# Linear attention into a routed attention layer: the last 64 tokens' values and scores by other shapes, and the whole program in another order

## The chip, the cores and the metric

The kernel runs on one core of a Trainium2 chip. The core has TensorE (PE in the profile, its weight loads PEld), VectorE (DVE), ScalarE (ACT), GpSimd (POOL), and SyncE (SP), which here issues all transfers. The metric is the device time of one execution in microseconds (us); of three runs the median counts.

## The reference

There are 8 batches of 576 tokens and 8 heads of 64. First comes a linear attention per head, with a feature map of 64 to 128, taken with both signs:

```python
def phi(x):
    proj = np.einsum('bhsd,df->bhsf', x, w_phi)
    proj = proj - np.max(np.abs(proj), axis=-1, keepdims=True)
    return np.concatenate([np.exp(proj), np.exp(-proj)], axis=-1)
q_p, k_p = (phi(q), phi(k))
kv = np.einsum('bhsf,bhsd->bhfd', k_p, v)
z = np.sum(k_p, axis=2)
num = np.einsum('bhsf,bhfd->bhsd', q_p, kv)
den = np.einsum('bhsf,bhf->bhs', q_p, z)[..., None] + 1e-06
return (num / den).astype(np.float32)
```

The heads' results side by side are x, 576 x 512 per batch. Then four experts of causal softmax attention (head width 64, scores scaled by 1/8) run on x, each with its own wq, wk, wv and wo. A token's result is the sum of its two best experts' outputs by `x @ w_gate`, weighted by a softmax over those two. All is float32.

## The kernel before

**Work.** Heads are handled in 32 pairs p (4 per batch), experts in two pairs g per batch b. A pair's queries and keys are projected with both heads' rows in the two halves of the array (`stream_q`, `stream_k`; the last 64 keys of both heads in `stream_tail`). Keys are centred on VectorE by their largest absolute value (`center`: a maximum and a subtraction) and turned into exponentials on ScalarE (`ek`). `stream_kv` sums keys by values into `kv`: 4 products (2 heads x 2 signs) of 65 columns (64 values and a one, for z), each over 5 blocks of tokens, in two 64-row halves. The fifth block holds the last 64 tokens of both heads, one head's in the upper partitions and the other's in the lower, and the values of the other head are zeros. Queries get their maximum from a POOL reduction (`phi_q`), a subtraction on VectorE and two exponentials on ScalarE; `stream_n` multiplies them by `kv`, `divide` divides, and `turn_x` transposes the quotients by way of memory into x.

**High and low parts.** x, the weights, q, k and y are kept as two float32r numbers, high and low, and a product is three: high by high, high by low, low by high. `proj_t` makes q and k of the expert pair g (`evac_q`, `evac_k`), `proj_v` the values and the gate's logits of all experts in 5 blocks of 128 tokens, the fifth of 64; `scores` the transposed scores in four steps n, 36 matmuls over 64 rows in all; `soft` masks them, copies them to `st`, and takes maxima; `post` subtracts and exponentiates them and multiplies by the values; `norm_y` and `move_y` scale and transpose; `project_out` (wo) and `store` end the batch. The key tile `kk2` is 640 columns wide, 64 of them zeros that `zeros` writes.

**Order.** Each of these is a generator of steps. `Plan.loop` walks through the string `PICKS`, two characters a step: the first picks the generator that goes on, the second the PSUM bank (of 8) that it gets, or, for a copy that ScalarE or VectorE can do, the engine. So `PICKS` sets every engine's order and the engine of every copy; each engine then works its own queue in that order and waits on semaphores. `keep_warm` issues matmuls of a constant, whose results nobody reads, in groups of three.

## Time and profile before

| | |
|---|---|
| runs | 564.62, 565.3, 569.82 us; median 565.3 |
| profiled execution | span 563.5 us, from the first to the last instruction; its time is not listed apart from the span, and the median stands 1.8 us above it |
| TensorE | busy 551.8 us (98%), weight loads 518.7 |
| VectorE | 492.9 us (87%) |
| ScalarE | 391.2 us (69%) |
| POOL | 192.7 us (34%) |
| DMA | 69 MB, all engines about half busy |

Busy time counts an engine from an instruction's start to its end; TensorE's matmuls are pipelined, so that several are open at once, and what one costs is the distance from its start to the next one's. A row `x16` merges that many instructions of a kind that follow each other. A float32 matmul of the code is two instructions in the profile, a float32r or bfloat16 one is one. Line 180 is the helper of the 128-row matmuls, line 407 that of the half-width ones, lines 189 and 202 the two engines' copies; there the names of the tiles tell the place.

### The profile page before, as it was taken

To read this page: it belongs to the slowest core of one execution; us is meant where nothing else is said; L and a number is where in the kernel's file an instruction comes from. 1 tells how busy PE (TensorE), PEld (TensorE's weight loads), DVE (VectorE), ACT (ScalarE), POOL (GpSimd) and SP (SyncE) were. 2 spreads that over 40 slices of the span, in tenths; PEclk is the share of its full clock that TensorE was granted. 3 is DMA by queue.
4 is the path that set the end of the run, shared out by engine and by line. 5 is a ranking of instruction groups with operands and counts; after the bars stand their busy time and mean duration, and the time that the engine had idled before them with its cause. 6 is when DMAs were issued, how large, how long until landed. Compare 5 with 4: busy or idle time off the path is not lost.

```text
span 563.5 us, 22862 instructions
## 1 busy us (share of the span) xinstructions
PE 551.8 (98%) x9704; PEld 518.7 (92%) x9704; DVE 492.9 (87%) x1245; ACT 391.2 (69%) x737; POOL 192.7 (34%) x78
## 2 busy tenths in 40 slices
PE   8999899999999999999999999999999999999996
PEld 6888799999999999999999999999999999999996
DVE  5799988999998999898878998899988998896992
ACT  3978757877956666897755784877785865574673
POOL 4565082244220555233203525083522310202320
PEclk9999999999999999999999999999999999999999
DMA  6577655555554636526545644356553253414222
GB/s 169 145 186 200 171 153 118 154 124 122 150 133 102 181 87 177 140 71 180 126 93 141 163 144 98 85 136 170 141 112 65 62 134 80 112 47 105 66 85 85
DMA packets 124757, 70.63 MB, mean 125 GB/s; under 512 B 81520, under 2 KB 107504, under 8 KB 124656
## 3 DMA queue, kind: packets, MB, share of 16 engines
q1 hardware_dynamic: 124656, 69.18, 48.7%
q8 instruction: 76, 1.25, 1.0%
q14 instruction: 25, 0.20, 0.1%
HBM read 46.15 MB, written 23.00 MB: 123 GB/s over the span
## 4 chain that ended last, share of the span: by engine, by line
PE 88%; DVE 8%; ACT 2%; issue 1%; DMA 0%; SPq 0%; DVEq 0%; ACTq 0%
PE ps_c L180 39%; PE ps_c L407 30%; PE ps_c L359 11%; PE ps_c L626 7%; DVE st L744 1%; DVE pmax L393 1%; DVE ek L395 1%; ACT ek L191 1%; DVE u L508 1%; DMA wf<-in_wts_dram 0%; DVE xt L540 0%; DVE xq L438 0%; DVE kv L202 0%; ACT u L189 0%; DVE u L202 0%
## 5 line engine op out<-in xcount | busy, mean ns | idle before, releaser
L498 POOL PARTITION_ALL_REDUCE mx<-u x32 | 127.0, 3993 | 113.7 <-ACT u L189 74.3
L180 PE MATMUL ps_c<-xh,qk 128*128 128x320 f32 (+1 forms) x512 | 106.3, 299 | 0.2 <-ACT st L189 0.2
L191 ACT ACTIVATE ek<-ek 128x1152 f32<-128x1152 f32 x64 | 74.8, 1169 | 26.4 <-DVE ek L395 25.5
L180 PEld LDWEIGHTS ps_c<-xh,qk 128*128 128x128 f32 x512 | 83.2, 189 | 1.8 <-ACT st L189 0.5
L498 POOL PARTITION_ALL_REDUCE tops<-top x15 | 54.2, 3611 | 82.9 <-DVE top L658 70.5
L407 PEld LDWEIGHTS ps_c<-v_in,ek 128*64 128x64 f32 x2560 | 77.4, 137 | 5.1 <-issue 2.6
L407 PE MATMUL ps_c<-v_in,ek 128*64 128x65 f32 x2560 | 81.4, 222 | 0.5 <-ACT ek L191 0.4
L180 PE MATMUL ps_c<-xl,qk 128*128 128x256 f32 (+1 forms) x256 | 75.8, 296 | 0.0
L189 ACT COPY st<-ps_c 128x288 f32<-128x288 f32 (+1 forms) x120 | 51.4, 505 | 25.1 <-DVE ps_c L646 16.7
L407 PE MATMUL ps_c<-kv,mx 128*64 128x65 f32 x1152 | 62.5, 224 | 3.3 <-DVE kv L202 2.6
L744 DVE TENSOR_TENSOR st<-st,tops 128x1152 f32<-128x1152 f32 (+4 forms) x75 | 57.7, 826 | 4.5 <-POOL tops L498 4.4
L393 DVE TENSOR_REDUCE pmax<-ps_c 128x4 f32<-128x512 f32 (+1 forms) x96 | 51.1, 546 | 11.0 <-PE ps_c L407 5.6
L407 PE MATMUL ps_c<-kv,u 128*64 128x65 f32 x1152 | 59.5, 221 | 0.0
L180 PE MATMUL ps_c<-vg,xh 128*128 128x260 f32 (+1 forms) x320 | 59.0, 285 | 0.0
L407 PEld LDWEIGHTS ps_c<-kv,mx 128*64 128x64 f32 x1152 | 48.1, 137 | 8.0 <-DVE kv L202 1.9
L189 ACT COPY u<-ps_c 128x320 f32<-128x320 f32 (+3 forms) x125 | 42.6, 416 | 17.2 <-PE ps_c L359 15.2
L395 DVE TENSOR_TENSOR ek<-ps_c,pmax 128x512 f32<-128x512 f32 (+1 forms) x96 | 51.9, 553 | 2.8 <-issue 0.5
L191 ACT ACTIVATE st<-st 128x1152 f32<-128x1152 f32 (+3 forms) x60 | 48.5, 865 | 7.0 <-DVE st L744 6.6
L180 PE MATMUL ps_c<-yh,wo 128*128 128x256 f32 (+1 forms) x256 | 52.1, 298 | 0.0
L180 PEld LDWEIGHTS ps_c<-xl,qk 128*128 128x128 f32 x256 | 48.5, 189 | 0.1
L407 PE MATMUL ps_c<-vl,st 128*64 128x65 f32 x1500 | 47.6, 222 | 0.8 <-ACT st L191 0.7
L180 PEld LDWEIGHTS ps_c<-vg,xh 128*128 128x128 f32 (+1 forms) x320 | 47.6, 177 | 0.8 <-issue 0.3
(116 smaller groups left out, 1175.4 us busy)
## 6 DMA issues: line engine op xcount, KB each, us to landing
v_in<-in_v_dram SPq DMA_DIRECT2D x32, 320.0 KB, 4.1
q_in<-in_qt_dram SPq DMA_DIRECT2D x64, 144.0 KB, 3.5
xl<-xd SPq DMA_DIRECT2D x32, 288.0 KB, 3.1
out_dram<-ot SPq DMA_DIRECT2D x32, 288.0 KB, 2.9
k_in<-in_kt_dram SPq DMA_DIRECT2D x32, 160.0 KB, 3.4
...
xd<-xt SPq DMA_DIRECT2D x64, 64.0 KB, 2.1
```

The source lines that it names most:

```text
L180: nc.tensor.matmul(o, a, b, start=start, stop=stop, skip_group_check=True)
L189: nc.scalar.copy(o, i)
L191: nc.scalar.activation(o, i, func, **kw)
L359: nc.tensor.matmul(o, a, b, start=True, stop=True, skip_group_check=True)
L393: dve(n * 128, [mk], [pk]).tensor_reduce(out=m[:, us], in_=src, axis=AX.X, op=ALU.max, apply_absolute_value=True)
L395: dve(n * 128, [(f'ek{p % EKB}1', us.start)], [pk, mk]).tensor_tensor(out=ek2[p % EKB][:, 1, us, :], in0=src, in1=m[:, us].unsqueeze(2).to ...
L407: nc.tensor.matmul(o, a, b, start=start, stop=stop, skip_group_check=True)
L498: nc.gpsimd.partition_all_reduce(o, i, 128, op)
L508: dve(2 * S, [uk], [mk], port=True).tensor_tensor(out=U, in0=U, in1=M, op=ALU.subtract)
L626: nc.tensor.matmul(pp_[e][:, o:o + q1 - q0], kk2[k_][r, 128 * j:128 * j + 128], q2[q_][r, q0:q1], start=m == 0, stop=m == 2, skip_group_ch ...
L744: dve(2 * n, [sj[j]], [*key, mk], port=True).tensor_tensor(out=a, in0=a, in1=tops[x][0:m, :, 128 * j:], op=ALU.subtract)
```

## The change

- **Values of the last 64 tokens.** x's high and low parts now lie in one tile `xb`. Once the low part is there, SP copies its last 64 tokens, high and low side by side, into `xe`, 128 columns. The fifth value block multiplies `xe` by the weights' high and low parts, 8 matmuls over 128 rows in place of 12 over 64. The upper 64 rows of the result are the high part's, the lower 64 the low part's; `evac_v` copies the lower ones to `vlo` and adds on VectorE.
- **Kv product.** For the last block one matmul per sign and half takes both heads' values, 130 columns, into two places of the bank; the other head's zeros make it right.
- **Last scores.** Where only 64 keys are left, the weights are 64 columns wide, not 128; `kk2` loses its zeros, and `zeros` goes.
- **Warm-up.** 18 groups of three, each with a bank of its own, at fixed places of the order; the first four key projections stand behind certain groups.
- **Order.** `PICKS` is another string throughout.

```diff
@@ -30,7 +30,8 @@
 EKB = 2
 XT_RATE = 1.085
 IB = 2
-WARM = 0
+WARMS = 18
+WARM_AT = (7, 11, 14, 17)
 
 
 ORDER = (('p0', 'v0', 's0', 'p1', 's1'), ('p0', 's0', 'p1', 's1', 'v0'))
@@ -50,51 +51,51 @@
 PICKS = (
-    "BACACADAAAAAAAAAAAAAAAAAAAGRNANAGjNANANACAG1OAOAG5OAOAOABAAAFCPIPIEjQIPIPIPIEADANICACAAAAAAAAAAAAAAAAAAAAAAAAAAAAAG1PAPA"
...
+    "BABABABABABABABABABABABABADAAAGIOAGaBAFECAE1NIQAHAQABANANANAPAOAGPQAQAGQRAADPAADADOAADEAOIADDADjBAFPFyCAMAQASAMAEFRAJAPA"
...
 )
@@ -167,8 +168,10 @@
     done = plan.done
     plan.both = [pp.tile([128, 512], F32, name=f"ps_c{i}") for i in range(BANKS)]
     plan.free = set(range(BANKS))
+    warm = cp.tile([128, 128], BF16, name="warm")
+    nc.vector.memset(warm, 1.0)
     for t in plan.both:
-        nc.vector.memset(t[:, NJ * V1 - 1:NJ * V1], 0.0)
+        nc.vector.memset(t[:, NJ * V1 - 1:512], 0.0)
 
     def sb(name, shape, dt=F32):
         return cp.tile(shape, dt, name=name)
@@ -209,8 +212,6 @@
     def load(o, i, w, r=(), rate=90.0):
         nc.sync.dma_start(o, i)
 
-    warm = sb("warm", [128, 128], BF16)
-    nc.vector.memset(warm, 1.0)
     col, row = sb("col", [128, 128]), sb("row", [128, 32])
     nc.vector.memset(col[:, 0:1], 0.0)
     for k in range(7):
@@ -254,7 +255,9 @@
     xt = [sb(f"xt{i}", [128, 4, 32 * NJ]) for i in range(2)]
     for t in xq:
         nc.vector.memset(t[64:128, :, 128:160], 0.0)
-    xT = [[sb(f"x{p}{i}", [128, S], F32R) for p in "hl"] for i in range(PXB)]
+    xB = [sb(f"xb{i}", [128, 2, S], F32R) for i in range(PXB)]
+    xT = [[t[:, n] for n in range(2)] for t in xB]
+    xE = sb("xe", [128, NP, 128], F32R)
 
     st = [[sb(f"st{n}", [128, 2, w]) for n, w in enumerate((S, 512, 512))], [u[n][:, :, 0:w] for n, w in enumerate((S, 512, 512))]]
     top, tops = [sb("top", [128, 2, S]), mx[0]], [sb("tops", [128, 2, S]), mx[1]]
@@ -265,11 +268,12 @@
     for t in yq:
         nc.vector.memset(t[64:128, :, 128:160], 0.0)
     q2 = [sb(f"q{p}", [128, S], F32R) for p in "hl"]
-    kk2 = [sb(f"kk{p}", [128, KC], F32R) for p in "hl"]
+    kk2 = [sb(f"kk{p}", [128, S], F32R) for p in "hl"]
     vl = sb("vl", [128, NJ, 4, 66])
     nc.vector.memset(vl[:, :, :, 65:66], 1.0)
     nc.vector.memset(vl[64:128, NJ - 1], 0.0)
     lg = vl[:, :, :, 0]
+    vlo = sb("vlo", [64, 4, 65])
     ge = sb("ge", [128, 5, 4, 4])
     gt, gs = sb("gt", [128, 3, 5, 4]), sb("gs", [128, 2, 5])
     gw = sb("gw", [128, 5, 4])
@@ -325,19 +329,13 @@
     w_vg = split_w("vg", WVG, [ot[1]], wts[:, c_vg:c_vg + WVG], 520)
     w_wo = split_w("wo", WO, [ot[0]], wts[:, c_vg + WVG:])
 
-    def zeros():
-        for x in kk2:
-            yield Step('POOL')
-            nc.gpsimd.memset(x[:, S:KC].bitcast(F32), 0.0)
-        done.add(('w', 4))
-
     def keep_warm():
-        pk, ps = yield Step('PE', (), 'c')
-        while ('x', WARM, 0) not in done:
-            yield Step('PE')
+        for n in range(WARMS):
+            t = yield Step('PE', (), 'c')
             for _ in range(3):
-                mm(ps[:, 0:128], warm, warm, True, True, 128, pk, [])
-        plan.release('c', (pk, ps))
+                mm(t[1][:, 0:128], warm, warm, True, True, 128, t[0], [])
+            plan.release('c', t)
+            done.add(('warm', n))
 
     def load_k():
         for p in range(NPAIRS):
@@ -361,7 +359,7 @@
     def stream_k():
         for p in range(NPAIRS):
             x, need = k_in[p % IB], [(f'k_in{p % IB}', n) for n in range(2)] + ['wphi']
-            k0, k1, pp_ = yield Step('PE', need, 'c', lambda: ('load_k', p) in done and ('w', 0) in done, tiling=(64, 128), n=3)
+            k0, k1, pp_ = yield Step('PE', need, 'c', lambda: ('load_k', p) in done and ('w', 0) in done and (p >= len(WARM_AT) or ('warm', WARM_AT[p]) in done), tiling=(64, 128), n=3)
             for n in range(4):
                 for h, pk in enumerate((k0, k1)):
                     r = slice(64 * h, 64 * h + 64)
@@ -455,14 +453,15 @@
             i = p % EKB
             ek, ekk = ek2[i], [f'ek{i}0'] + [(f'ek{i}1', t) for t in (0, 4, 8)]
             kc, ps = yield Step('PE', ekk + [vk], 'c', lambda: ('phi_k', p) in done and ('load_v', p) in done, tiling=(128, 64))
-            for h in range(2):
-                for c in range(2):
+            for c in range(2):
+                for h in range(2):
                     o = V1 * (2 * h + c)
-                    for t in range(NJ):
-                        u_ = 4 * h + t if t < 4 else 8
+                    for t in range(4):
                         for m in range(0, 128, 64):
-                            column_mm(ps[m:m + 64, o:o + V1], ek[:, c, u_, m:m + 64], v_in[:, 4 * h + t if t < 4 else 8 + h, :],
-                                       t == 0, t == 4, kc, ekk + [vk])
+                            column_mm(ps[m:m + 64, o:o + V1], ek[:, c, 4 * h + t, m:m + 64], v_in[:, 4 * h + t, :], c + h + t == 0, False, kc, ekk + [vk])
+                for m in range(0, 128, 64):
+                    to = ps[m:m + 64, 0:4 * V1].rearrange("p (h c x) -> p h c x", h=2, c=2)[:, :, c]
+                    nc.tensor.matmul(to, ek[:, c, 8, m:m + 64], v_in[:, 8:10, :], start=False, stop=True, skip_group_check=True)
             done.add(('kv', p))
             st = Step(copies(4 * V1), [kc], pred=has('num', p - 2) if p > 1 else None, hot=True)
             yield st
@@ -556,6 +555,9 @@
         sub_lo(S, lo, lo.bitcast(F32), hi, f'xl{i}', [*xr, f'xh{i}'])
         for s0, s1 in PARTS:
             done.add(('x', p, s0))
+        yield Step('SP', [f'xl{i}'], pred=(lambda: ('pe', p // NP - 1) in done) if p >= NP else None)
+        load(xE[:, p % NP].rearrange("f (n s) -> f n s", n=2).bitcast(F32), xB[i][:, :, 512:S].bitcast(F32), 'xe')
+        done.add(('xe', p))
 
     def all_x(*ps):
         return lambda: all(('x', p, q_[0]) in done for p in ps for q_ in PARTS)
@@ -606,7 +608,13 @@
         def evac_v(j, m, kc, ps):
             st = Step(copies(260), [kc], hot=True)
             yield st
-            copy(st.eng, 260, vl[:m, j, :, 0:65], ps[:m, 0:260].rearrange("p (n d) -> p n d", d=65), [f'vs{j}'], [kc])
+            src = ps[:, 0:260].rearrange("p (n d) -> p n d", d=65)
+            if m == 128:
+                copy(st.eng, 260, vl[:, j, :, 0:65], src, [f'vs{j}'], [kc])
+            else:
+                copy(st.eng, 260, vlo, src[64:128], ['vlo'], [kc])
+                yield Step('DVE', [kc], hot=True)
+                nc.vector.tensor_tensor(out=vl[0:64, j, :, 0:65], in0=src[0:64], in1=vlo, op=ALU.add)
             plan.release('c', (kc, ps))
             done.add(('v', b, j))
 
@@ -623,7 +631,8 @@
                     for m, (q_, k_) in enumerate(((0, 0), (0, 1), (1, 0))):
                         for e, pk in enumerate((k0, k1)):
                             r = slice(64 * e, 64 * e + 64)
-                            nc.tensor.matmul(pp_[e][:, o:o + q1 - q0], kk2[k_][r, 128 * j:128 * j + 128], q2[q_][r, q0:q1],
+                            n_ = min(128, S - 128 * j)
+                            nc.tensor.matmul(pp_[e][0:n_, o:o + q1 - q0], kk2[k_][r, 128 * j:128 * j + n_], q2[q_][r, q0:q1],
                                              start=m == 0, stop=m == 2, skip_group_check=True)
                 for e, pk in enumerate((k0, k1)):
                     plan.spawn(soft(g, n, blocks, e, pk, pp_[e]))
@@ -666,17 +675,17 @@
             wvg = wsp["vg"]
             for j in range(NJ):
                 m = min(128, S - 128 * j)
-                kc, ps = yield Step('PE', [k for c in xk for k in c], 'c', has('av', b - 1, 1) if b else has('w', 2))
-                n = 0
-                for c in range(4):
-                    for x_, w_ in ((0, 0), (0, 1), (1, 0)):
-                        mm(ps[:m, 0:260], xs[c][x_][:, 128 * j:128 * j + m],
-                           wvg[w_][:, c * 260:(c + 1) * 260], n == 0, n == 11, 260, kc,
-                           [xk[c][x_], ('vg', w_)])
-                        n += 1
+                kc, ps = yield Step('PE', (), 'c', lambda: ('w', 2) in done and (not b or ('av', b - 1, 1) in done) and (j < NJ - 1 or all(('xe', NP * b + c) in done for c in range(NP))))
+                parts = [(xs[c][x_][:, 128 * j:128 * j + m], c, w_) for c in range(4) for x_, w_ in ((0, 0), (0, 1), (1, 0))]
+                if m < 128:
+                    parts = [(xE[:, c], c, w_) for c in range(4) for w_ in range(2)]
+                for n, (x_, c, w_) in enumerate(parts):
+                    mm(ps[:, 0:260], x_, wvg[w_][:, c * 260:(c + 1) * 260], n == 0, n == len(parts) - 1, 260, kc, [])
+                if m < 128:
+                    done.add(('pe', b))
                 plan.spawn(evac_v(j, m, kc, ps))
 
-        yield Step('PE', (), None, lambda: all_x(*range(b * NP, b * NP + NP))() and all(('w', i) in done for i in (0, 1, 4)))
+        yield Step('PE', (), None, lambda: all_x(*range(b * NP, b * NP + NP))() and all(('w', i) in done for i in (0, 1)))
         for part in ORDER[b == B - 1]:
             yield Step('PE')
             g = int(part[-1])
@@ -862,7 +871,7 @@
         load(out[b, 128 * t:128 * t + 128, :], ot[t % 2], ('out', b, t), oks)
         done.add(('out', 4 * b + t))
 
-    for gen in (load_phi(), keep_warm(), zeros(), load_k(), load_q(), load_v(), stream_k(), stream_tail(), stream_q(), weights(w_qk, ('w', 1)), weights(w_vg, ('w', 2)), weights(w_wo, ('w', 3)), stream_kv(), stream_n(), stream_s()):
+    for gen in (load_phi(), keep_warm(), load_k(), load_q(), load_v(), stream_k(), stream_tail(), stream_q(), weights(w_qk, ('w', 1)), weights(w_vg, ('w', 2)), weights(w_wo, ('w', 3)), stream_kv(), stream_n(), stream_s()):
         plan.spawn(gen)
     plan.loop()
     in_order(tc, plan.behind)
```

What the string moves, at three places. TensorE at the start of the program, before (`q_in` and `k_in` are queries and keys of the first two pairs, in two buffers; the 64x128 rows are the last 64 keys):

```order
L359 MATMUL ps_c_65<-q_in_109,wf 128x256
L359 MATMUL ps_c_66<-q_in_110,wf 128x320
L359 MATMUL ps_c_67<-q_in_110,wf 128x320
L359 MATMUL ps_c_62<-q_in_110,wf 128x256
L359 MATMUL ps_c_68<-q_in_110,wf 128x256
L180 LDWEIGHTS warm
L180 MATMUL ps_c_61<-warm 128x128
...
L407 MATMUL ps_c_63<-wf,k_in_107 64x128 x2
L359 MATMUL ps_c_64<-wf,k_in_107 128x128
```

and now:

```order
L357 MATMUL ps_c_64<-q_in_109,wf 128x256
L405 MATMUL ps_c_65<-wf,k_in_107 64x128 x2
L357 MATMUL ps_c_66<-wf,k_in_107 128x128
...
L357 MATMUL ps_c_67<-wf,k_in_107 128x128
L357 MATMUL ps_c_68<-q_in_110,wf 128x320
L357 MATMUL ps_c_62<-q_in_110,wf 128x320
L357 MATMUL ps_c_61<-q_in_110,wf 128x256
L357 MATMUL ps_c_63<-q_in_110,wf 128x256
L183 LDWEIGHTS warm
```

The first pair's keys came after the second pair's queries and three warm-up matmuls; now they come before them.

TensorE at the end of one batch's value projection, before (`vg` are the value and gate weights, `xh` and `xl` x's parts, the 64-row results the fifth block):

```order
L180 MATMUL ps_c_64<-vg,xh_154 64x260 x2
L180 MATMUL ps_c_64<-vg,xl_155 64x260
L180 MATMUL ps_c_64<-vg,xh_156 64x260 x2
L180 MATMUL ps_c_64<-vg,xl_157 64x260
L180 MATMUL ps_c_64<-vg,xh_146 64x260 x2
L180 MATMUL ps_c_64<-vg,xl_147 64x260
L180 MATMUL ps_c_64<-vg,xh_148 64x260 x2
L180 MATMUL ps_c_64<-vg,xl_149 64x260
```

and now, at the end of another batch's:

```order
L183 MATMUL ps_c_65<-vg,xb_146 128x260 x3
L183 MATMUL ps_c_65<-vg,xb_147 128x260 x3
L183 MATMUL ps_c_65<-vg,xb_148 128x260 x3
L183 MATMUL ps_c_65<-vg,xb_149 128x260 x3
L183 MATMUL ps_c_68<-vg,xe 128x260 x8
```

Twelve matmuls of the fifth block became eight, from one tile.

VectorE in the third batch, now, around the fifth value block and a group of scores (lines 205 are copies, 655 the masks, 667 the maxima, 507 the queries' subtraction, 617 the new addition):

```order
L205 COPY vl<-ps_c_64 128x4x65
L205 COPY vl<-ps_c_63 128x4x65
L655 TENSOR_TENSOR ps_c_61<-ps_c_61,mask 128x128
L655 TENSOR_TENSOR ps_c_65<-ps_c_65,mask 128x128
L205 COPY vlo<-ps_c_62 64x260
...
L205 COPY st_155<-ps_c_63 128x512
L667 TENSOR_TENSOR top<-ps_c_64,st_153 128x448
L507 TENSOR_TENSOR u_129<-u_129,mx_133 128x1152
...
L188 TENSOR_TENSOR xb_147<-xb_147 128x576
L617 TENSOR_TENSOR vl<-ps_c_62,vlo 64x4x65
```

Before, every copy of `vl`, `st` and `ot` stood on ScalarE; now 7 of 40, 15 of 120 and 17 of 64 stand on VectorE (and 14 more of `u`, 8 of `kkh`, 4 of x), 65 in all.

## Rows read from the trace of the kernel before

**Rows 1.** The page's first part: busy us, share of the span, instructions of each engine.

```profile
PE 551.8 (98%) x9704; PEld 518.7 (92%) x9704; DVE 492.9 (87%) x1245; ACT 391.2 (69%) x737; POOL 192.7 (34%) x78
```

**Rows 2.** Busy time by stretch: length, engines' busy us (instructions), granted clock, DMA share, GB/s.

```profile
0.00:10.00 10.00, 7.98 (x49) 5.86 (x50) 4.07 (x43) 4.08 (x9) 2.64 (x7) 1.00 0.61 161
20.00:80.00 60.00, 56.85 (x1267) 50.71 (x1264) 55.51 (x126) 47.67 (x74) 29.99 (x9) 1.00 0.68 178
30.00:60.00 30.00, 29.04 (x675) 25.61 (x675) 29.31 (x62) 24.41 (x38) 15.72 (x4) 1.00 0.74 187
80.00:500.00 420.00, 417.72 (x7517) 396.96 (x7517) 379.68 (x941) 297.27 (x561) 139.94 (x55) 1.00 0.50 123
500.00:563.00 63.00, 59.22 (x712) 56.64 (x710) 45.30 (x126) 36.03 (x84) 12.42 (x7) 1.00 0.30 86
```

**Rows 3.** What TensorE waited for: us in total, times, longest.

```profile
PE ps_c L450 <- DVE yq L438: 0.8, 1, 0.8
...
PE ps_c L359 <- DMA wf<-in_wts_dram: 0.7, 1, 0.7
```

**Rows 4.** TensorE's timeline, value blocks: start us, length, engine, line, operation, count.

```profile
86.21 0.41 PE L180 MATMUL ps_c<-vg,xh 128*128 128x260 f32 x2
86.45 0.29 PE L180 MATMUL ps_c<-vg,xl 128*128 128x260 f32 x1
86.58 0.40 PE L180 MATMUL ps_c<-vg,xh 128*64 128x260 f32 x2
...
87.89 0.28 PE L180 MATMUL ps_c<-vg,xl 128*64 128x260 f32 x1
```

**Rows 5.** TensorE's timeline, 64-column scores.

```profile
89.62 0.27 PE L626 MATMUL ps_c<-qh,kkl 64*128 64x64 f32 x2
89.73 0.28 PE L626 MATMUL ps_c<-ql,kkh 64*128 64x64 f32 x2
89.84 0.39 PE L626 MATMUL ps_c<-qh,kkh 64*128 64x320 f32 x2
```

**Rows 6.** Groups by form: count, busy us, mean ns, idle before and its releasers.

```profile
L407 PEld LDWEIGHTS ps_c<-v_in,ek 128*64 128x64 f32 x2560 | 77.4, 137 | 5.1 <-issue 2.6 <-ACT ek L191 0.5 <-ACT u L189 0.5
...
L646 DVE TENSOR_TENSOR ps_c<-ps_c,mask 128x128 f32<-128x128 f32 x128 | 31.6, 289 | 7.3 <-PE ps_c L626 6.4
...
L626 PEld LDWEIGHTS ps_c<-qh,kkh 64*128 64x128 f32 x192 | 19.8, 185 | 3.2 <-issue 1.1 <-ACT st L189 0.7 <-ACT vl L189 0.4
...
L202 DVE COPY u<-ps_c 128x320 f32<-128x320 f32 x5 | 2.2, 483 | 0.3 <-PE ps_c L359 0.3
L202 DVE COPY u<-ps_c 128x256 f32<-128x256 f32 x6 | 2.2, 416 | 0.0
```

**Rows 7.** TensorE's timeline, a kv product and a key projection.

```profile
17.73 2.55 PE L407 MATMUL ps_c<-v_in,ek 128*64 128x65 f32 x80
20.11 0.39 PE L407 MATMUL ps_c<-wf,k_in 128*64 128x128 f32 x4
...
90.68 1.08 PE L359 MATMUL ps_c<-wf,k_in 64*128 64x128 f32 x16
91.69 0.44 PE L407 MATMUL ps_c<-wf,k_in 128*64 128x128 f32 x4
```

**Rows 8.** TensorE's timeline, the start.

```profile
1.30 2.74 PE L180 MATMUL ps_c<-warm 128*128 128x128 bf16 x24 [1.30 <-DVE col L215]
4.76 4.21 PE L359 MATMUL ps_c<-q_in,wf 64*128 64x320 f32 x16 [0.72 <-DMA wf<-in_wts_dram]
...
10.98 2.52 PE L180 MATMUL ps_c<-warm 128*128 128x128 bf16 x42
```

**Rows 9.** VectorE's timeline: its first key maximum, and a run of masks.

```profile
10.09 0.29 DVE L393 TENSOR_REDUCE pmax<-ps_c 128x1 f32<-128x128 f32 x1 [4.34 <-PE ps_c L407]
...
90.12 1.73 DVE L646 TENSOR_TENSOR ps_c<-ps_c,mask 128x128 f32<-128x128 f32 x8 [0.83 <-PE ps_c L626]
```

**Rows 10.** DMA issues: queue, kind, count, KB each, median us to landing.

```profile
yl<-yd SPq DMA_DIRECT2D x56, 64.0 KB, 3.0
```

More of the change, by code (lines that the diff above doesn't have):

```diff
@@ new lines @@
+    "XAWAWAVAQAUAMAUAHAJAUARAUASAF6FOGAGANAPAPIDADAQAYAOASASABABAQAGAQATAPAJAEDKhXARATIJIKGVAGAVAVARAQAOASASAPAUAUAWAWAWAWAWA"
+    "WAGAKAKAKCKFTAUAVAVACAGAGASASAFPFmCALAWIWAVIUADQQANAFjTAF-QAVAUAGAWAMAVAVAVARAVAOAOANANALAGAKAAAQANAQAOAJBJEJAJDQASARARA"
+    "QAJGJHJDJAJARAJqDADAOAPADMSIQATARASAJ3SAQARASATAJQJrJAWAWAXATAYAWAYAUALALAOASAUAUASASASAQAUAKAJGXAKAUAJBJHSASAPATARAVARA"
+    "WAJEVAGAECRASAWARAPAAABAVAUADADASAAADIHFEDQAPABAHAPATARATANAQAMACARAQAQADAHCHAOALAAAOALAOAOAEGQADAOADsOAIBOAITOAOAVAPAPA"
@@ new lines @@
+    "QAQAQACAMAGAPAO3PAOAOADADAQAQAQAHFQASAAASASAOAQAQAOALARARIHAMAOAOIQAOAMAJAJcJ6JBXATAQAXASIWARARATAUARAOAI1QAOAUARAHDRATA"
+    "RATALATARATIEEVARAHAFXUARAVAFdFhVAUARAPAVAVAOATIJCUARAVARAUAD9FZaAOAUATAXATAZAUANANAXASAXASASAUAPARACADAJADAMAJANABABALA"
+    "GAD0MAQAJDJBJHJCTATAOAEAPAIlTAXAXAVAPAQALAVAVAHCVAVAUATATAPAOASAHASASASASISAFHVISIRAMAQASAFZSAFqFHVAAAUADAOAOAVAOADADMOA"
+    "OAEFOAIWXAQASACAHAAANAYAYAXAVABAKAJAVAHIUAUASANAN7UASAGASASISASIJBJAJEJFJGQAOADALADATARATAPATAMASATATAQATITARAMAQALAOACA"
@@ L98 @@
+    "CACAGADAEIEABABGEADADABECICAABADDICABAAHACDABABIBAAFAAAGABAAAIAAAIAAAA"
 )
```

79 lines of the change are left out of this document (35 added, 44 removed).

## The prediction

> **What bounds the kernel now.** I read the page's busy shares first, then the busy times by stretch, then what TensorE waits for, then the timeline at each place that the change edits, and last the durations by form. The busy shares [rows 1] put TensorE at 98% and VectorE at 87% of a span of 563.5 us. The stretches [rows 2] tell more: from 80 to 500 us TensorE is idle 2.28 us out of 420, while VectorE is busy 379.68 (90.4%) and ScalarE 297.27 (71%). From 30 to 60 us it is VectorE that is full (29.31 of 30 us, 97.7%) and TensorE that loses 0.96 us. TensorE's waits are small: two of the list [rows 3] matter below, and only 0.7 us in the whole run is for a transfer. So after the start each matmul that goes away shortens the run, as long as VectorE can follow.
>
> **Values of the last 64 tokens.** Before, 12 matmuls of 260 columns with 64-wide weights begin at 86.58, the last of them at 87.89 [rows 4]: 1.31 us for eleven steps, 0.119 each. After, 8 of 260 columns with 128-wide weights do the work (the fourth product, low by low, comes along unasked). The 128-wide ones just ahead, three from 86.21 to 86.58, take 0.123 each. So 12 x 0.119 - 8 x 0.123 = 0.45 us per batch, 3.6 us in 8 batches, all on TensorE's path. The rows fix this within 0.5 us.
>
> **Last scores.** The six 64-column matmuls of a group come in pairs; the second pair starts at 89.62, the third at 89.73, the next form at 89.84 [rows 5]: 0.11 us per pair, though 64 columns are a quarter of the 260 that take 0.12. The pair waits for its two weight loads. A 128-wide load lasts 185 ns, a 64-wide one 137 [rows 6]. I take these two pairs as half as long, which saves 0.11 us per group and 1.8 over 16 groups. Ends: 0 if it isn't the load that holds them, 2.6 if all 96 matmuls gain 27 ns. The Trainium skill ("TensorE: Matmul & The Clock Gate", Step-by-step) says that a load's time scales with its column count; by that rule alone all loads halve, the saving is the 2.6, and the total would be 0.8 us lower. The rows show 185 against 137, less than half off, and the rows decide.
>
> **Kv product.** Per pair of heads, 80 instructions of 65 columns (two for each matmul of the code) take 2.38 us, 17.73 to 20.11 [rows 7], 30 ns each. Now 64 of 65 columns and 8 of 130 do it. By columns nothing changes. The nearest wide row of the same number type is the key projection: 16 of 128 columns in 1.01 us, 90.68 to 91.69, 63 ns each [rows 7], so 130 columns cost 64, against 2 x 30: a loss of 4 ns x 8 x 32 = 1 us at one end. At the other, if the loads set the pace, 8 x 30 ns x 32 = 7.7 us less. I take 0, near the projection's row.
>
> **The start.** Of 126 warm-up matmuls 54 are left: 39 at first (24 before) and 15 later (102 before, in runs of 42, 3 and 6). A run of 42 takes 2.52 us [rows 8], 60 ns each: 87 fewer are 5.2 us. The 15 more at the front stand ahead of the transfer that TensorE waits for anyway (0.7 us [rows 3]). What counts is whether something was ready in their place. VectorE idles 4.34 us until 10.09 [rows 9], since the first key projection stands behind the second pair's queries; in the new order the keys come right after the first pair's queries, and their transfer is issued ahead of the second queries. The second pair's queries, half of the 4.21 us at 4.76 [rows 8], and three warm-ups stood between: some 2.5 us that VectorE, the full engine of 30 to 60 us, starts earlier. With a little of the warm-up runs I take 3.0. Ends 0 and 5.2.
>
> **The end.** TensorE sits 0.8 us for the last transposes' input [rows 3]. Six output matmuls now stand in front of the transposes and fill part of it: 0.6 us. Ends 0 and 0.8.
>
> **Transfers.** Each pair adds a 64 KB copy into the new tile, on SP, which waits there for the low parts from VectorE; input and x transfers stand behind it in that queue. A 64 KB one lands in 3.0 us [rows 10], and TensorE paid 0.7 us for transfers in all. Only the fifth value block needs the copies, after four others of 12 x 0.12 us. I cost them at nothing; if that cover fails, it is about 2 us once per batch. The two small clears on POOL that go away were done before TensorE had data.
>
> **VectorE is what gets dearer.** Counting both orders, 65 copies go from ScalarE to VectorE: 20 of 320 columns, 18 of 256, 11 of 288, 5 of 512, 7 of 260 and 4 casts of 576. VectorE's rows give 483 ns for 320 columns and 416 for 256 [rows 6]; by the slope between them, 1.05 ns a column, the others are 450, 684, 420 and 752. That is 31.5 us. The new sum of the two halves adds 8 operations and 2 copies of 260 columns, 4.2 us. Against it 19 small ones leave, 6.1 us by their means. Net 29.6 us in 56 more instructions, whose ends overlap the next by some 60 ns (eight masks of 289 ns [rows 6] run in 1.73 us [rows 9]): 26 to 30, taken as 27, since casts out of SBUF run shorter than the slope says. The 492.9 becomes 520.
>
> **The sum.** TensorE's side: 563.5 - 3.6 - 1.8 - 0 - 3.0 - 0.6 = 554.5 us of span. VectorE's side: by 500 us it has done 447.6 (492.9 less 45.3), 4.1 of it before 10 us [rows 2]. Of the 27, 24 fall here. So 467.5 us must go between about 7 us and 63 us before the end; on TensorE's side that is 484.5 us, a level of 96.5%. The rows have 97.7% where VectorE is full and 90.4% where it had time to spare. So it just fits, and I add 1.0 for TensorE's waits (the 0.96 lost in the full 30 us; ends 0, and 13 if 3.2% were lost throughout, as from 30 to 60). Span 555.5. The runs' median, 565.3, stands 1.8 above this execution's span, so the forecast is **557 us**, 1.5% under the median.
>
> **Rivals.** *VectorE's level eats the gain.* The span is 467.5 / level + 70. At 95.8% the time is 559.6, where faster by 1% ends; at 95% it is 564, at 94.6% 566. For it: each engine works its queue in order, and from 20 to 80 us VectorE reached only 92.5% on average [rows 2]. Against it: much of that stretch is the start, where TensorE had warm-ups and little to feed VectorE with. Chance 0.27, 560 to 571.
>
> *VectorE's late copies stall TensorE, and the run gets slower.* The score, value and output copies that now queue on VectorE behind subtractions of 1152 columns hold PSUM banks, and the next matmuls wait for a bank. At the 92.5% of 20 to 80 us the span is 575 and the time 577. It decides from 93.7% downward. Against it: 105 of 120 score copies stay on ScalarE, which is 71% busy. Chance 0.07.
>
> *More is gained:* the start gives 5.2 and part of the kv loads' 7.7 comes true. Time 545 to 551, chance 0.08.
>
> *The clock falls.* The granted clock is 1.00, the 2.4 GHz level, in each stretch [rows 2]; but the first 24 warm-ups took 2.74 us and 42 later ones 2.52 [rows 8]. Without warm-ups after the first ones, the start's waits lie open as idle time. At half the clock some 20 us of matmuls there would cost up to 10 more: 567, chance 0.03. The Trainium skill's same page (HAM oscillation) says that gaps between bursts of matmuls drop the array to half its clock; no row here shows a fall before the tail.
>
> That the 64-wide loads save nothing moves the time by 1.8 only.
>
> **How the numbers follow.** The forecast, 551 to 559.6, has 0.55. One per cent is about what a measurement of this kernel can tell from no change; it ends at 559.6 and 571. Faster: 0.55 + 0.08 = 0.63. Same: 0.27 + 0.03 = 0.30. Slower: 0.07. The range reaches from 549 (half of the extra gain) to 566 (VectorE at 94.6%) and leaves out some 0.17.
>
> **What would show it.** Right: the last value block's eight matmuls in 0.98 us, the 64-column score pairs 0.055 apart, the first key maximum on VectorE before 8 us, VectorE near 520 us busy and over 96% from 20 us to 60 before the end, TensorE idle under 4 us from 80 to 490. Wrong: TensorE's waits for copies of VectorE or ScalarE over 6 us in sum, a granted clock below 1.00 before the tail, or VectorE well under 96% while TensorE isn't full.

## The result, and the profile after

The changed kernel takes 547.3 us (median of 4 runs, 545.87 to 549.14) against 565.6 for the kernel before: a ratio of 0.9666, with a 95% interval from 0.9626 to 0.9706. The forecast was 557, from 549 to 566. The direction was right, but 18 us came off where 8 were forecast. The profiled execution took 546.13 us with a span of 544.3.

The page's first part, against [rows 1]:

```profile
PE 532.4 (98%) x9344; PEld 506.3 (93%) x9344; DVE 501.5 (92%) x1301; ACT 373.6 (69%) x689; POOL 192.6 (35%) x76
```

TensorE is again at 98%, though the span is 19 us shorter: that share told nothing of what could be gained. VectorE has 501.5 us and not the 520 of the forecast. The busy times by stretch, against [rows 2]:

```profile
0.00:10.00 10.00, 8.71 (x88) 7.47 (x89) 8.05 (x49) 3.35 (x7) 2.29 (x5) 1.00 0.60 169
20.00:80.00 60.00, 57.69 (x1195) 53.34 (x1191) 54.49 (x117) 48.82 (x86) 35.47 (x9) 1.00 0.75 188
30.00:60.00 30.00, 28.77 (x750) 26.54 (x744) 27.40 (x65) 28.02 (x45) 13.42 (x5) 1.00 0.80 200
80.00:480.00 400.00, 395.73 (x7134) 380.08 (x7136) 375.82 (x975) 280.26 (x515) 136.81 (x54) 1.00 0.52 130
```

From 30 to 60 us VectorE is no longer the full engine: 27.40 us busy where it had 29.31, and ScalarE has 28.02 where it had 24.41. From 80 to 480 us VectorE is at 94.0% and TensorE idle for 4.27 us. The start on TensorE's timeline, against [rows 8]:

```profile
1.29 4.32 PE L183 MATMUL ps_c<-warm 128*128 128x128 bf16 x39 [1.29 <-DVE ps_c L174]
5.54 1.38 PE L357 MATMUL ps_c<-q_in,wf 64*128 64x320 f32 x8
6.84 0.44 PE L405 MATMUL ps_c<-wf,k_in 128*64 128x128 f32 x4
7.21 1.16 PE L357 MATMUL ps_c<-wf,k_in 64*128 64x128 f32 x16
8.21 1.14 PE L357 MATMUL ps_c<-q_in,wf 64*128 64x320 f32 x8
9.28 1.01 PE L183 MATMUL ps_c<-warm 128*128 128x128 bf16 x15
```

and VectorE's first maximum, against [rows 9]:

```profile
7.63 0.28 DVE L391 TENSOR_REDUCE pmax<-ps_c 128x1 f32<-128x128 f32 x1
```

The maximum comes at 7.63 us instead of 10.09, as forecast. The last value block and the 64-column scores, against [rows 4, 5]:

```profile
78.79 1.13 PE L183 MATMUL ps_c<-vg,xe 128*128 128x260 f32 x8
79.85 0.40 PE L635 MATMUL ps_c<-qh,kkh 64*128 64x288 f32 x2
...
82.25 0.21 PE L635 MATMUL ps_c<-qh,kkh 64*64 64x64 f32 x2
82.28 0.24 PE L635 MATMUL ps_c<-qh,kkl 64*64 64x64 f32 x2
82.33 0.24 PE L635 MATMUL ps_c<-ql,kkh 64*64 64x64 f32 x2
82.39 0.41 PE L635 MATMUL ps_c<-qh,kkh 64*128 64x320 f32 x2
```

The block's eight matmuls take 1.06 us (0.98 forecast); three score pairs take 0.14 us, 0.03 to 0.06 apart (0.055 forecast).

A first view of where the time went is the first expert projection, the first work that needs a whole batch of x. Its first row in the kernel before, and in the changed one:

```profile
74.29 0.38 PE L180 MATMUL ps_c<-xh,qk 128*128 128x256 f32 x1
```

```profile
62.36 0.86 PE L183 MATMUL ps_c<-xb,qk 128*128 128x256 f32 x5
```

It starts 11.9 us earlier. From there to the end the spans leave 489.2 us before and 481.9 after. So of 19.2 us of span, 11.9 lie ahead of that projection and 7.3 behind it. A mark like this depends on what an order puts ahead of it: the first scores, a little later, come only 8.2 us earlier (88.09 and 79.85), and the part on the prediction goes by them.

### The profile page after: what moved, and what is told of

It reads as the page before. It is cut to its first block, busy times and chain, and to the rows that moved or that the text cites. A ratio compares the mean times of both kernels' runs of the same rounds, so it can differ in the third digit from the quotient of the medians.

```text
span 544.3 us, 22196 instructions
## 1 busy us (share of the span) xinstructions
PE 532.4 (98%) x9344; PEld 506.3 (93%) x9344; DVE 501.5 (92%) x1301; ACT 373.6 (69%) x689; POOL 192.6 (35%) x76
## 4 chain that ended last, share of the span: by engine, by line
PE 83%; DVE 6%; DMA 5%; ACT 2%; SPq 2%; issue 1%; DVEq 0%; ACTq 0%
PE ps_c L183 38%; PE ps_c L405 26%; PE ps_c L357 11%; PE ps_c L635 7%; DMA xb<-xd 3%; PE ps_c L464 2%; SPq L213 2%; DMA xd<-xt 1%; DVE u L507 1%; DVE u L753 1%; DMA q_in<-in_qt_dram 1%; DVE pmax L391 1%; DVE ek L393 1%; DVE st L753 0%; ACT st L192 0%
## 5 line engine op out<-in xcount | busy, mean ns | idle before, releaser
L183 PE MATMUL ps_c<-xb,qk 128*128 128x256 f32 (+1 forms) x768 | 107.0, 297 | 0.5 <-DVE xb L188 0.4
L183 PEld LDWEIGHTS ps_c<-xb,qk 128*128 128x128 f32 x768 | 102.2, 188 | 2.7 <-DVE xb L188 0.9
L405 PE MATMUL ps_c<-v_in,ek 128*64 128x65 f32 x2048 | 72.0, 222 | 2.2 <-issue 1.4
L405 PEld LDWEIGHTS ps_c<-v_in,ek 128*64 128x64 f32 x2048 | 67.8, 137 | 4.4 <-issue 1.8
L192 ACT COPY st<-ps_c 128x288 f32<-128x288 f32 (+1 forms) x105 | 47.7, 506 | 24.6 <-DVE ps_c L655 17.8
L192 ACT COPY u<-ps_c 128x320 f32<-128x320 f32 (+3 forms) x111 | 40.7, 411 | 18.0 <-PE ps_c L357 16.8
L405 PEld LDWEIGHTS ps_c<-kv,u 128*64 128x64 f32 x1152 | 48.2, 138 | 0.0
L183 PE MATMUL ps_c<-vg,xb 128*128 128x260 f32 x384 | 48.0, 284 | 0.0
L183 PEld LDWEIGHTS ps_c<-vg,xb 128*128 128x128 f32 x384 | 46.7, 188 | 0.7 <-DVE ek L393 0.3
L405 PEld LDWEIGHTS ps_c<-vl,st 128*64 128x64 f32 x1500 | 45.6, 138 | 0.9 <-issue 0.6
```

What stands on the lines that cost most here:

```text
L183: nc.tensor.matmul(o, a, b, start=start, stop=stop, skip_group_check=True)
L192: nc.scalar.copy(o, i)
L405: nc.tensor.matmul(o, a, b, start=start, stop=stop, skip_group_check=True)
```

## The experiments

Each was timed beside the kernel before on the same chip; ratios are to that, with their 95% intervals, and a ratio need not be that of two medians. "Old order" is the string of steps of the kernel before, "new order" that of the changed one.

| kernel | us | ratio |
|---|---|---|
| changed kernel | 547.3 | 0.9666 (0.9626 to 0.9706) |
| new order, no edit of matmuls | 554.3 | 0.9784 (0.9741 to 0.9828) |
| old order, all three edits | 591.3 | 1.0476 (1.0432 to 1.0520) |
| new order, old kv | 550.1 | 0.9726 (0.9684 to 0.9767) |
| new order, old last scores | 549.8 | 0.9721 (0.9676 to 0.9767) |
| new order, old value block | 546.8 | 0.9663 (0.9619 to 0.9708) |
| old order, new kv and scores | 563.3 | 0.9966 (0.9927 to 1.0005) |
| old order, edits, sum on VectorE | 588.1 | 1.0395 (1.0345 to 1.0445) |
| the same, copies on GpSimd's queue | 566.6 | 1.0012 (0.9986 to 1.0038) |
| old order, edits, copies late | 605.2 | 1.0697 (1.0621 to 1.0772) |
| old order, 24 warm-ups | 568.6 | 1.0053 (1.0022 to 1.0083) |
| old order, keys first | 565.5 | 1.0003 (0.9967 to 1.0039) |
| old order, keys first, fewer warm-ups | 565.7 | 0.9999 (0.9973 to 1.0024) |
| new order, keys late | 548.7 | 0.9700 (0.9664 to 0.9736) |
| new order, 85 more warm-ups | 552.8 | 0.9788 (0.9748 to 0.9827) |
| new order, 15 fewer warm-ups | 548.0 | 0.9666 (0.9630 to 0.9702) |
| new order, 42 copies back on ScalarE | 557.4 | 0.9857 (0.9787 to 0.9926) |
| new order, score copies back | 553.8 | 0.9785 (0.9732 to 0.9837) |
| old order, the same 42 copies on VectorE | 589.2 | 1.0413 (1.0374 to 1.0453) |

**The order without the edits.** All three hunks on matmuls are undone; of each the core:

```diff
-                    for t in range(4):
+                    for t in range(NJ):
...
-                            n_ = min(128, S - 128 * j)
+                            n_ = 128
...
-                if m < 128:
-                    parts = [(xE[:, c], c, w_) for c in range(4) for w_ in range(2)]
```

> The new order with its warm-ups, but the old five-block kv product, 128-wide last scores and twelve-matmul last value block. Theory A (the order gives most of it, through the start): TensorE gets 7.1 us of matmuls back (kv 0.8, values 3.9, scores 2.5, by the spacing of the two traces), so 554 to 556 us, and the first expert projection still starts near 62 us. Theory B (the order gives what the prediction gave it, 3.6 us, the edits the rest): 561 to 563 us. Theory C (VectorE has taken over as the bound, matmuls are hidden): 547 to 549 us.

554.3 us, as in theory A. The order alone takes 12.2 us off by the ratio (9.7 to 14.6 by its interval; 10.6 by the medians, 9.1 by the spans of the two profiled executions), and the first expert projection starts at 63.52:

```profile
63.52 0.86 PE L183 MATMUL ps_c<-xb,qk 128*128 128x256 f32 x5
```

**The edits without the order.** The same three hunks, put into the kernel before; the 64 KB copy right behind the subtraction, the sum right behind the copy of the other half:

```diff
         sub_lo(S, lo, lo.bitcast(F32), hi, f'xl{i}', [*xr, f'xh{i}'])
+        load(xE[:, p % (2 * NP)]..., xB[i][:, :, 512:S].bitcast(F32), 'xe')
...
+                copy(st.eng, 260, vlo, src[64:128], ['vlo'], [kc])
+                nc.vector.tensor_tensor(out=vl[0:64, j, :, 0:65], in0=src[0:64], in1=vlo, op=ALU.add)
```

> The old order with all its 126 warm-ups, and the three edits (kv, last scores, last value block; the copies into the new tile have two sets of slots). Theory A: 7.1 us less matmul work, all on TensorE's path after the start, 557.5 to 559.5 us; the first expert projection still starts near 74 us. Theory B: the edits give 14 to 15 us, 550 to 552 us. Theory C (the old order can't use them, since VectorE is late at the start): 563 to 566 us.

No theory had this: 591.3 us, 26 slower. TensorE's list of waits in this run:

```profile
PE ps_c L409 <- DMA v_in<-in_v_dram: 4.1, 1, 4.1
PE ps_c L409 <- ACT kv L189: 3.2, 2, 2.7
PE ps_c L361 <- DMA q_in<-in_qt_dram: 3.0, 1, 3.0
```

and of SyncE's:

```profile
SPq L210 <- DVE xb L185: 40.1, 9, 11.3
```

SyncE stands 40.1 us for the low parts, and loads of values and queries come late. The granted clock is 0.98 here, where it was 1.00. Four runs followed this up.

**Kv and scores alone in the old order.**

```diff
-                    for t in range(NJ):
+                    for t in range(4):
...
+                            kk2[k_][r, 128 * j:min(S, 128 * j + 128)]
```

> The kernel before with the new kv product and the 64-column last scores, but its own last value block. The edits alone came out 26 us slower in the old order; this tells which of them does it. If the value block does (its copies, its sum of two halves): kv 0.8 and scores 2.5 us of matmuls go away on TensorE's path, 561 to 563 us. If any shortening of matmuls throws the old order out of step: over 573 us.

563.3 us, a gain of 1.9 whose interval still touches no change: of the three edits it is the value block, with its copies and its sum placed as here, that brings the loss.

**The sum without a wait for ScalarE.**

```diff
-                copy(st.eng, 260, vlo, src[64:128], ['vlo'], [kc])
+                copy('DVE', 260, vlo, src[64:128], ['vlo'], [kc])
```

> All three edits in the old order, the copies into the new tile behind the subtractions; of the last value block both halves go out on VectorE, so its sum waits for no copy of ScalarE. If VectorE's wait for that copy (7.9 us in six waits in the run of the edits alone) made the old order slow: 557 to 562 us. If the copies on SyncE's queue did, or the longer work on VectorE: 575 us or more.

588.1: VectorE's wait for the other half was at most a small part of it (3.2 us by the medians; the two intervals just overlap).

**The copies on another queue**, with the edit just shown kept:

```diff
-        load(xE[:, p % (2 * NP)]..., xB[i][:, :, 512:S].bitcast(F32), 'xe')
+        nc.gpsimd.dma_start(xE[:, p % (2 * NP)]..., xB[i][:, :, 512:S].bitcast(F32))
```

> All three edits in the old order, both halves of the last value block out on VectorE, and the 64 KB copies into the new tile issued from GpSimd's queue instead of SyncE's, so that the loads of values, queries and x stand behind no wait for VectorE. If SyncE's queue is what makes the old order lose (TensorE waits 4.1 us for values and 3.0 for queries in it): 558 to 563 us. If GpSimd now waits in its place (its maxima come later): 575 us or more.

566.6 us, 21.5 less by this line alone, though above the 558 to 563 expected. GpSimd stands for the low parts in SyncE's place (69.0 us in 12 waits), and neither loads of values nor of queries are in TensorE's list any more. The queue that waits for the low parts is shown as the cause. A part of the loss goes by way of the clock: its mean was 0.985 in the profiled execution of the run just shown and is 1.00 here, at most some 9 us by an estimate (0.015 of 587). That the edits still gain nothing here is not explained.

**The copies later on SyncE**, all four at the batch's first value block:

```diff
+                if j == 0:
+                    for c in range(NP):
+                        load(xE[:, (b * NP + c) % (2 * NP)]...)
```

> All three edits in the old order again, but the four 64 KB copies of a batch are issued together at its first value block, not each behind the subtraction that makes the low part. If the copies held up SyncE's queue (SyncE waits there for VectorE, loads of values and queries stand behind it): 557 to 561 us, and TensorE's waits for transfers under 1.5 us. If the sum of the two halves is the cause (VectorE waits there for a copy that stands in ScalarE's queue): 583 to 592 us.

A miss, 605.2: now the transfer itself is late, and the last block waits for it.

```profile
PE ps_c L180 <- DMA xe<-xb: 24.9, 5, 10.4
```

**Old kv product in the new order.**

```diff
-                    for t in range(4):
+                    for t in range(NJ):
```

> The changed kernel with the old kv product: five blocks of 65 columns per head and half instead of four and one of 130. By TensorE's spacing 0.8 to 1.8 us more, 548 to 549 us; at the forecast's price of nothing 547.3; if the weight loads set the pace, 7.7 more, 555 us.

**Old last scores in the new order.**

```diff
-    kk2 = [sb(f"kk{p}", [128, S], F32R) for p in "hl"]
+    kk2 = [sb(f"kk{p}", [128, KC], F32R) for p in "hl"]
...
-                            n_ = min(128, S - 128 * j)
+                            n_ = 128
```

> The changed kernel with 128-wide last scores (keys padded with zeros to 640). By the forecast's price 1.8 us more, 549; by TensorE's spacing 2.5 to 4.0, 550 to 551 us. If the value block's result repeats (3.9 us of matmuls that cost nothing in the whole): 546.5 to 548 us.

**Old value block in the new order.**

```diff
-                if m < 128:
-                    parts = [(xE[:, c], c, w_) for c in range(4) for w_ in range(2)]
...
-        load(xE[:, p % NP]..., xB[i][:, :, 512:S].bitcast(F32), 'xe')
```

> The changed kernel with the old last value block: twelve matmuls on 64 columns of x, no copies into the new tile, no sum of halves; the order is the same otherwise. By TensorE's spacing 3.9 to 4.6 us more, 551 to 552 us. If VectorE's relief (4.2 us of copy and sum less) outweighs it: 545 to 547 us.

Undone singly they cost 2.7, 2.5 and -0.5 us by the medians, all three undone together 7.0. An interval of one is some 3 us to either side, so only the three together are settled: they are near the 5.4 forecast. The value block, the largest of the forecast's edits (3.6), shows no gain of its own.

**Keys first, in the old order.** The order's rows on TensorE:

```diff
-L359 MATMUL ps_c_66<-q_in_110,wf 128x320
-L359 MATMUL ps_c_67<-q_in_110,wf 128x320
...
 L407 MATMUL ps_c_68<-wf,k_in_107 64x128 x2
 L359 MATMUL ps_c_66<-wf,k_in_107 128x128
...
+L359 MATMUL ps_c_62<-q_in_110,wf 128x320
+L359 MATMUL ps_c_63<-q_in_110,wf 128x320
```

> The kernel before with one piece of its order changed: the first pair's keys (their transfer, their matmuls, VectorE's maxima and subtractions of them) stand ahead of the second pair's queries; all 126 warm-ups stay. If this is the start's gain: VectorE's first maximum near 7.5 us instead of 10.1, the first expert projection 2.5 to 3 us earlier, 562 to 563 us. If it carries all of the start's 9 to 11 us: 555 to 557 us. If the 42 warm-ups that follow hide it: 565 us.

VectorE's first maximum comes at 6.71 us, 3.4 earlier, the first expert projection 2 us earlier, and the time is the same. The piece of the start on which the forecast rested shows no gain by itself; the interval leaves room for 1.9 us, less than the 2.5 that were given to it.

**Keys late, in the new order**: the same rows the other way round.

```diff
-L405 MATMUL ps_c_65<-wf,k_in_107 64x128 x2
...
+L357 MATMUL ps_c_66<-q_in_110,wf 128x320
```

> The changed kernel with the first pair's keys put back behind the second pair's queries (their matmuls and their transfer), banks dealt out anew for it; nothing else moves. If the early keys are worth what the prediction gave them: VectorE's first maximum 2 to 3 us later, the first expert projection at 64 to 65 us, 549.5 to 551 us. If they are worth nothing, as in the old order: 547 to 548 us.

548.7: 1.4 us, between the two cases and inside the intervals.

**Fewer warm-ups, old order.**

```diff
-            for _ in range(3):
+            for _ in range(3 if n <= 8 else 0):
```

> The kernel before with only the first 24 of its 126 warm-up matmuls; nothing else changes. If the warm-ups stood in the way of ready work: 102 x 60 ns = 6.1 us less, 559 to 560 us. If they only filled waits of the start (VectorE sets it): 564.5 to 566 us, with TensorE idle where they stood. If the clock falls in those gaps: granted clock under 1.00 before 80 us and 567 to 575 us.

The third case: 568.6, 0.5% slower, with two falls of the granted clock. Busy times by stretch in this run, and TensorE's timeline at the second fall:

```profile
68.00:70.00 2.00, 0.38 (x4) 0.00 (x0) 0.00 (x0) 1.01 (x2) 0.00 (x0) 1.00 0.23 53
70.00:72.00 2.00, 0.27 (x5) 0.30 (x7) 1.60 (x3) 1.80 (x4) 0.00 (x0) 0.67 0.02 8
72.00:74.00 2.00, 2.00 (x42) 2.00 (x41) 2.00 (x7) 0.52 (x2) 0.00 (x0) 0.50 0.71 200
74.00:76.00 2.00, 2.00 (x38) 1.88 (x36) 1.36 (x4) 1.14 (x4) 0.77 (x1) 0.50 0.61 155
76.00:78.00 2.00, 2.00 (x20) 1.97 (x22) 0.19 (x1) 0.00 (x0) 2.00 (x1) 0.62 0.59 133
78.00:80.00 2.00, 2.00 (x15) 1.04 (x13) 2.00 (x4) 1.63 (x6) 2.00 (x2) 1.00 0.67 197
```

```profile
71.73 0.70 PE L409 MATMUL ps_c<-kv,mx 128*64 128x65 f32 x8 [3.35 <-ACT mx L191]
```

After 3.35 us of idle the clock stands at 0.50, the 1.2 GHz level, for some 7 us, and the projection comes at 79.94.

**Keys first and 42 warm-ups, old order.**

```diff
-            for _ in range(3):
+            n += 1
+            for _ in range(3 if n <= 9 or n % 6 == 0 else 0):
```

> The kernel before with the first pair's keys ahead of the second pair's queries, as in the run before, and with 42 warm-ups instead of 126: the first 27, and three in every sixth step after them (order otherwise unchanged). If early keys and the warm-ups' absence together are the start's gain: the first expert projection at 66 to 69 us, 557 to 560 us. If the old order needs its warm-ups: granted clock under 1.00 in a stretch before 80 us, projection at 74 us or later, 565 us or more.

565.7, the second case: the granted clock from 20 to 40 us is 0.91, and the projection comes at 75.06. In the old order the 84 warm-ups that are gone here neither cost nor gave time.

**More warm-ups, new order.**

```diff
-            for _ in range(3):
+            for _ in range(3 if n < 13 else 20):
```

> The changed kernel with 20 warm-up matmuls instead of 3 in each of its five later warm-up steps, 85 more. If they delay ready work: 85 x 60 ns = 5.1 us more, 552 to 553 us. If VectorE or transfers set the start: under 1 us, 547 to 548.5 us.

**No later warm-ups, new order.**

```diff
-            for _ in range(3):
+            for _ in range(3 if n < 13 else 0):
```

> The changed kernel without its 15 later warm-ups (the first 39 stay). If each costs what the 85 added ones cost (65 ns): 546.4 us, 0.9 less. If the clock needs them: granted clock under 1.00 before 40 us and 549 to 553 us.

85 more cost 5.5 us, as expected at 60 ns each; 15 fewer gain nothing (548.0, granted clock 1.00). So in the new order matmuls are ready where the added warm-ups stand. That the old one had none there is argued from the run with 24 warm-ups, which lost time though it left 102 out.

**The copies back on ScalarE.**

```diff
-            copy(st_.eng, w, st[x][d_][:, e, c0:c0 + w], ps[:, 0:w], [key[n]], [pk])
+            copy('ACT', w, st[x][d_][:, e, c0:c0 + w], ps[:, 0:w], [key[n]], [pk])
...
-        copy(st.eng, s1 - s0, o[:, s0:s1], ps[:, 0:s1 - s0], [ok], [pk])
+        copy('ACT', s1 - s0, o[:, s0:s1], ps[:, 0:s1 - s0], [ok], [pk])
```

> The changed kernel with the 41 copies of scores, values and outputs that VectorE took over made by ScalarE again, some 19 us by VectorE's durations; the order is the same. If VectorE's load is what holds the changed kernel: 540 to 544 us. If the copies were put where VectorE is free and ScalarE isn't: matmuls wait for banks, 550 to 556 us. If neither engine holds it: 546.5 to 548.5 us.

557.4, 10 us slower, though VectorE has less to do, and ScalarE is busy for 70% only. The copies are 42, not the 41 of the expectation: VectorE has 1259 instructions for the changed kernel's 1301. The page's first part:

```profile
PE 536.4 (97%) x9344; PEld 508.0 (91%) x9344; DVE 487.0 (88%) x1259; ACT 387.1 (70%) x731; POOL 192.4 (35%) x76
```

TensorE's list now has waits for ScalarE's copies of outputs and values that the changed kernel's list hasn't:

```profile
PE ps_c L405 <- ACT ot L192: 1.6, 2, 1.3
...
PE ps_c L357 <- ACT vl L192: 1.3, 1, 1.3
PE ps_c L405 <- ACT vl L192: 1.1, 1, 1.1
```

**The score copies alone back**: the first pair of lines of that diff.

> The changed kernel with the 16 score copies alone made by ScalarE again; outputs and values stay with VectorE. If the gain of the moved copies is in the scores (TensorE's spacing there was 4.9 of the 11.5 us lost when all moved back): 551 to 553 us. If it is in outputs and values: 547 to 549 us.

553.8: some 6.5 of the 10 us are in 16 copies of scores (some 3 to either side).

**The same copies on VectorE in the old order**; `SCORES`, `OUTS` and `VALUES` list the changed kernel's 42.

```diff
-            copy(st_.eng, w, st[x][d_][:, e, c0:c0 + w], ps[:, 0:w], [key[n]], [pk])
+            copy('DVE' if (b, g, n, e) in SCORES else st_.eng, w, st[x][d_][:, e, c0:c0 + w], ps[:, 0:w], [key[n]], [pk])
```

> The kernel before with the same 42 copies (16 of scores, 17 of outputs, 9 of values) made by VectorE that the changed kernel gives it; nothing else moves. If VectorE's help is worth by itself what it was worth in the new order (10 us): 555 to 557 us. If it pays only in an order made for it: 564 to 567 us. If VectorE's queue, full with longer work there, holds the banks (the forecast's fear): 568 us or more.

589.2, 24 us slower, worse than the forecast's rival of late copies (577). TensorE's waits are short and many; the first two:

```profile
PE ps_c L410 <- ACT st L194: 3.4, 2, 2.9
PE ps_c L410 <- DVE kv L205: 2.0, 3, 1.1
```

The mean granted clock was 0.991 in the profiled execution, an estimated 5 us of the 24 at most. So a copy's engine is right or wrong only together with the order around it. No order was made anew for a kernel of these runs: what the old copies could do in an order fitted to them, or the edits in one fitted to them alone, is not known.

## Why the prediction missed the size

The forecast took 2.6 us for the order (start 3.0, end 0.6, less 1.0 for VectorE) and 5.4 for the edits. The runs give 12.2 for the order (9.7 to 14.6) and, from the two ratios with it, 6.7 for the edits (some 3 to either side). **The miss is the order's, and two steps failed: "The start. ... I take 3.0. Ends 0 and 5.2", and VectorE's "it just fits, and I add 1.0".**

The first projection alone would put 10.8 us of the order's gain into the start (74.29 to 63.52). But the new order puts off work that then stands between the two halves of that projection: with the order alone, queries and keys from 66.89 to 71.16. The first scores come behind all of it. Their first rows in the kernel before, with the order alone, and in the new order with the 42 copies back on ScalarE:

```profile
88.09 0.40 PE L626 MATMUL ps_c<-qh,kkh 64*128 64x288 f32 x2
```

```profile
81.70 0.40 PE L632 MATMUL ps_c<-qh,kkh 64*128 64x288 f32 x2
```

```profile
81.00 0.40 PE L635 MATMUL ps_c<-qh,kkh 64*128 64x288 f32 x2
```

| one profiled execution each, us | to the first scores | from there to the end |
|---|---|---|
| kernel before | 88.1 | 475.4 |
| new order, no edit of matmuls | 81.7 | 472.7 |
| changed kernel | 79.9 | 464.4 |
| changed kernel, 42 copies back | 81.0 | 474.8 |

The start gives 6.4 us by the order alone and 8.2 in the changed kernel, more than the forecast's upper end. The larger part, 11.0 us, lies behind the first scores, and 10.4 of it is gone when the copies go back. Without the edits that part is 2.8: it takes the edits and the copies on VectorE together. These are marks of single executions, that of the order alone the slowest of its six, so a us or two of each is open.

**The start.** The step looked only at the instructions that it had names for: the warm-ups and the first keys. What it left out shows in the two traces ahead of the first projection, in groups of equal instructions (VectorE's, then TensorE's: count, busy us, mean ns, idle before) and in the stretch's busy times. Before:

```profile
L508 DVE TENSOR_TENSOR u<-u,mx 128x1152 f32<-128x1152 f32 x8 | 12.2, 1523 | 0.4 <-POOL mx L498 0.3
...
L540 DVE STREAM_TRANSPOSE xt<-xq 128x640 f32<-128x640 f32 x6 | 5.0, 835 | 0.4 <-ACT xq L191 0.4
...
L359 PE MATMUL ps_c<-q_in,wf 64*128 64x320 f32 (+1 forms) x88 | 16.2, 474 | 0.9 <-DMA wf<-in_wts_dram 0.7
L180 PE MATMUL ps_c<-warm 128*128 128x128 bf16 x126 | 9.8, 239 | 1.3 <-DVE col L215 1.3
```

```profile
0.00:74.29 74.29, 69.12 (x1439) 59.42 (x1439) 63.66 (x168) 53.23 (x85) 34.58 (x15) 1.00 0.66 172
```

After:

```profile
L507 DVE TENSOR_TENSOR u<-u,mx 128x1152 f32<-128x1152 f32 x7 | 9.4, 1338 | 0.6 <-POOL mx L497 0.6
L539 DVE STREAM_TRANSPOSE xt<-xq 128x640 f32<-128x640 f32 x5 | 4.1, 831 | 1.6 <-ACT xq L194 1.5
...
L357 PE MATMUL ps_c<-q_in,wf 64*128 64x320 f32 (+1 forms) x72 | 11.6, 427 | 0.3 <-DMA q_in<-in_qt_dram 0.3
L183 PE MATMUL ps_c<-warm 128*128 128x128 bf16 x54 | 5.3, 287 | 1.3 <-DVE ps_c L174 1.3
```

```profile
0.00:62.36 62.36, 58.78 (x1279) 52.52 (x1279) 53.87 (x148) 48.12 (x77) 30.99 (x12) 1.00 0.80 194
```

A batch needs four pairs of x. The old order had put six transposes of x, eight subtractions of queries and 88 query matmuls (eight a pair) ahead of the first projection, more than the first batch needs; the new one has five, seven and 72. VectorE's busy time there falls by 9.8 us and TensorE's by 10.3, of which 4.5 are warm-ups and 4.6 queries. The matmuls put off are paid later, a part of them at once, between the halves of the projection. The experiments show that the new order as a whole does this, and that its two named pieces don't (keys first 0, fewer warm-ups +0.5%, both together 0). That its warm-ups could go because there was work in their place fits these runs. How the start's gain splits between VectorE's work and TensorE's was read from the traces and not tested.

One term that the step put at nothing has a size too: "The 15 more at the front stand ahead of the transfer that TensorE waits for anyway." Before, the sixteen query matmuls behind the first 24 warm-ups lasted 4.21 us [rows 8], the next sixteen 2.64:

```profile
13.43 2.64 PE L359 MATMUL ps_c<-q_in,wf 64*128 64x320 f32 x16
```

In the changed kernel, behind 39 warm-ups, the first eight last 1.38 and the next eight 1.14. So some 1.6 us go with the longer front, by these rows, against queries that start 0.8 us later (5.54 and 4.76); the profile's clock column gives 1.00 for both starts, and no run changed the front alone.

**VectorE.** "Taken as 27 ... 520 ... it just fits, and I add 1.0" was wrong in size and in sense. VectorE's busy time rose by 8.6 us. The durations were right (482 ns for 320 columns, 483 in [rows 6]): added up, they rose by 22.9 us. But the busy share counts overlapping instructions once, and the overlap grew by the rest. The forecast took 60 ns of it an instruction, where its own rows give 83 (eight times 289 ns in 1.73 us). The same 42 copies cost 17.9 us of busy time in the old order (492.9 to 510.8). And the copies that were priced as a burden are a gain of 10 us in the new order, nearly all of it behind the first scores, with neither engine full: ScalarE was at 70% with them, and TensorE waited for it. A sum of durations against a share of the span can't see this; by the waits, what counts is whether the queue is free when the bank must be.

**Values, scores, kv, end.** The durations forecast for the value block, the scores and kv held: 1.06 us, 0.05 a pair, and 2.40 us a product against 2.39 (medians of the two traces). The end wasn't tested apart. The transfers "at nothing" held in the new order (0.7 us of waits for values). What the forecast named beside them is real in the old order: loads behind SyncE's wait for the low parts cost 21.5 us, and the late copy that it priced at 2 us a batch made TensorE wait 24.9 us in five waits.

**The signs named beforehand.** Right: the maximum before 8 us, the block, the score pairs, clock 1.00, waits for copies under 6 us. Wrong: VectorE at 501.5 us, and at 93.6% from 20 us to 60 before the end, and TensorE idle 4.28 us from 80 to 490 where under 4 was said. "VectorE well under 96% while TensorE isn't full" was the sign against the forecast's sum; the trace shows its first half, with TensorE at 99.0% in that stretch. The rival "more is gained" (545 to 551, chance 0.08) has the time and half of the reason: the start gave more than its 5.2, but the kv product is no shorter. That the copies on VectorE would be a gain was in no rival.

The Trainium skill ("Perfetto Trace Analysis", Identifying the Most-Contended Engine) says that the share of time with a matmul running is a poor measure of how close TensorE is to its limit, and to take the arithmetic done against the peak and the weight loads' share instead. The trace agrees on the poor measure (98% in both kernels); the weight loads' share moved from 92% to 93% and would not have told of 18 us either. The arithmetic against the peak wasn't worked out.
